# Attention over 256 heads: the last 32 query rows packed four heads to a tile, V through a staging copy, P·V metered by credits

## The chip, the core and the metric

The kernel runs on one core of a Trainium2 chip. A core has TensorE (PE in the profile; PEld is its weight load), VectorE (DVE), ScalarE (ACT), GpSimd (POOL) and SyncE (SP), which issues the DMAs here. Operands lie in SBUF, matmul results in PSUM, which has eight banks. The metric is the device time of one execution in microseconds; lower is better.

## The reference

```python
# q [8, 32, 1312, 128], k and v [8, 32, 512, 128], bf16
scale = q.shape[-1] ** -0.5
scores = jnp.einsum("bhqd,bhkd->bhqk", q, k) * scale
p = _softmax(scores, axis=-1)
return jnp.einsum("bhqk,bhkd->bhqd", p, v)
```

There are 8 x 32 = 256 independent heads, each with 1312 queries, 512 keys and a head dimension of 128.

## The kernel before

`fast_path` does all the work in a normal run. It goes through the heads in groups of eight (G = 8, 32 groups). The scores are computed transposed, keys on the partitions: for each of the four chunks of 128 keys (`c`), three matmuls of 512, 512 and 288 query columns (L145) with the transposed K chunk as weight write a score tile of 128 x 1312 over three PSUM banks; ScalarE takes the exponential of all of it, with a fixed shift instead of the row maximum, into the bf16 tile `pT` (L146). There are two such score tiles (six banks).

The second product, P·V, uses 128 columns of `pT` as weight and a chunk of V with a column of ones beside it (129 columns, tile `vp`) as the moving operand. Four chunks add up, so the output tile has 128 queries x 128 features and, in the column of ones' place, the softmax denominator. A head has eleven query tiles: ten cover queries 0 to 1279, the eleventh covers the last 128 queries, 96 of which the tenth tile has too; only its last 32 rows are stored. That makes 44 matmuls of 129 columns a head (L161). Tiles are gathered in groups, (0,1,2), (3,4,5), (6,7,8), (9,10), each in one of the two PSUM banks of the pool `ps_o`. After a group VectorE takes the reciprocal of the denominators into R (L165) and multiplies them into the output tile `om` (L167, L169) or, for the eleventh tile, `ol` (L170). At a group's end `check_group` counts the denominators that are in range.

The program is laid out by slots, four to a head. In slot s the code emits the scores and exp of chunk s mod 4 of head s div 4, and then eleven matmuls of P·V of the head that began five slots earlier (PV_LAG, PV_PER_SLOT; the generator `pv_steps`). A scheduler then sets the final order of each engine: it follows the code where everything is at hand, and takes a later instruction where it reckons that the next one must wait.

Loads go by SyncE's queue, in an order that `sp_dma` fixes. At a group's first slot `load_T` issues the next group's K, as one transposing DMA from rows of 128 elements (L100), and its Q for queries 0 to 1279, one transposing DMA a head (L110). Some slots later `load_plain` issues the 32 left-over query rows of the group after next, four heads to a tile (L73), and its V (L86), and the finished group's outputs are stored (L180, L182). The left-over rows are turned by two PE transposes a group into columns 1280 to 1311 of `qT` (L134, L135). V goes by DMA straight into `vp`, and GpSimd sets the column of ones (L83). kT and qT have two buffers, vp three.

After the heads `validity_flag` sums the counts; `exact_loop` redoes heads only if a denominator was out of range, which does not happen with these inputs.

Of the kernel before, what the change touches and what calls it, by code (L numbers as in the profile page):

```python
# [10 lines left out]
FP32 = mybir.dt.float32  # L11
# [5 lines left out]
AX = mybir.AxisListType  # L17

D, SQ, SK = 128, 1312, 512
NT = 11  # L20
QMAIN = 1280
QRANGES = ((0, 512), (512, 512), (1024, 288))
GROUPS = [(0, 1, 2), (3, 4, 5), (6, 7, 8), (9, 10)]
TILE_COL = [t * 128 for t in range(10)] + [SQ - 128]
# [3 lines left out]
P_FLUSH = 1.0e-20  # L28
G = 8


NOSYNC = mybir.DependencyInfo(mybir.DependencyClass.NoSync, mybir.DependencyReason.DATA)
PV_LAG = 5
PV_PER_SLOT = 11
QL = SQ - QMAIN
VW = 136
LB = 128 // QL


def fast_path(tc, qf, kf, vf, of, ident, R, CNT, NH):  # L40
# [4 lines left out]
    NLB = G // LB  # L45
    with ExitStack() as ctx:
        qpool = ctx.enter_context(tc.tile_pool(name="qT", bufs=2))
        kpool = ctx.enter_context(tc.tile_pool(name="kT", bufs=2))
        vpool = ctx.enter_context(tc.tile_pool(name="vpool", bufs=3))
        lpool = ctx.enter_context(tc.tile_pool(name="lpool", bufs=3))  # L50
        ptp = ctx.enter_context(tc.tile_pool(name="ptp", bufs=3))
        outp = ctx.enter_context(tc.tile_pool(name="outp", bufs=3))
        olp = ctx.enter_context(tc.tile_pool(name="olp", bufs=3))
        ps_s = ctx.enter_context(tc.tile_pool(name="ps_s", bufs=2, space=bass.MemoryType.PSUM))
        ps_o = ctx.enter_context(tc.tile_pool(name="ps_o", bufs=2, space=bass.MemoryType.PSUM))
        jpool = ctx.enter_context(tc.tile_pool(name="jpool", bufs=2))
        grp = {}
        st = {}
        pending_stores = []
        last_dma = [None]  # L60

# [13 lines left out]

        def load_V(g, j0=0, j1=G):
            if g >= NG:
                return
            h0 = g * G
            d = grp.setdefault(g, {})  # L80
            if "vp" not in d:
                vp = vpool.tile([128, G, 4, VW], BF16, tag="vp", name=f"vp{g}")
                nc.gpsimd.memset(vp[:, :, :, D:D + 1], 1.0)  # L83
                d["vp"] = vp
            vp = d["vp"]
            sp_dma(nc.sync.dma_start(vp[:, j0:j1, :, 0:D].rearrange("p j c d -> p (j c) d"),  # L86
                                     vf[h0 + j0:h0 + j1].rearrange("h (c p) d -> p (h c) d", c=4)))

        def load_plain(g):
            load_left(g)  # L90
            load_V(g)

        def load_K(g, j0=0, j1=G):
            if g >= NG:
                return
            h0 = g * G
            d = grp.setdefault(g, {})
            if "kT" not in d:
                d["kT"] = kpool.tile([128, G, SK], BF16, tag="kT", name=f"kT{g}")
            sp_dma(nc.sync.dma_start_transpose(d["kT"][:, j0:j1, :], kf[h0 + j0:h0 + j1].rearrange("h s d -> (h s) d")))  # L100

        def load_Q(g, j0=0, j1=G):
            if g >= NG:
                return
            h0 = g * G
            d = grp.setdefault(g, {})
            if "qT" not in d:
                d["qT"] = qpool.tile([128, G, SQ], BF16, tag="qT", name=f"qT{g}")
            for j in range(j0, j1):
                sp_dma(nc.sync.dma_start_transpose(  # L110
                    d["qT"][:, j, 0:QMAIN].rearrange("d (t p) -> d t p", t=10),
                    qf[h0 + j, 0:QMAIN, :].rearrange("(p t) d -> p (t d)", t=10)))

        def load_T(g):
            load_K(g)
            load_Q(g)

        def check_group(g):
            rg = R[:, g * G * NT:(g + 1) * G * NT]
            junk = jpool.tile([128, G * NT], FP32, tag="junk", name=f"junk{g}")  # L120
            nc.vector.tensor_scalar(junk[:], rg, R_LO, None, ALU.is_ge, ALU.add, accum_out=CNT[:, 2 * g:2 * g + 1])  # L121
            junk2 = jpool.tile([128, G * NT], FP32, tag="junk", name=f"junkb{g}")
            nc.vector.tensor_scalar(junk2[:], rg, R_HI, None, ALU.is_le, ALU.add, accum_out=CNT[:, 2 * g + 1:2 * g + 2])  # L123

        def flush_stores():
            for fn in pending_stores:
                fn()
            pending_stores.clear()

        def left_transpose(g):  # L130
            d = grp[g]
            tps = ps_o.tile([128, G * QL], BF16, tag="o", name=f"tl{g}")
            for b in range(NLB):
                nc.tensor.transpose(tps[:, b * 128:(b + 1) * 128], d["ql"][:, b, :], ident[:])  # L134
            nc.vector.tensor_copy(d["qT"][:, :, QMAIN:SQ], tps[:].rearrange("d (h i) -> d h i", h=G))  # L135

        def qk_exp(h, c):
            g, j = divmod(h, G)
            gd = grp[g]
            d = st.setdefault(h, {})  # L140
            if c == 0:
                d["pT"] = ptp.tile([128, 4, SQ], BF16, tag="pT", name=f"pT{h}")
            s = ps_s.tile([128, 3 * 512], FP32, tag="s", name=f"s{h}_{c}")
            for (q0, qn_) in QRANGES:
                nc.tensor.matmul(s[:, q0:q0 + qn_], lhsT=gd["kT"][:, j, c * 128:(c + 1) * 128], rhs=gd["qT"][:, j, q0:q0 + qn_], start=True, stop=True)  # L145
            nc.scalar.activation(d["pT"][:, c, :], s[:, 0:SQ], Exp, scale=scale, bias=-T0)  # L146

        def pv_steps(h):
            g, j = divmod(h, G)
            gd = grp[g]  # L150
            d = st[h]
            if j == 0:
                gd["om"] = outp.tile([128, G, 10, D], BF16, tag="om", name=f"om{g}")
                gd["ol"] = olp.tile([128, G, D], BF16, tag="ol", name=f"ol{g}")
            om = gd["om"]
            for gi, tl in enumerate(GROUPS):
                ng = len(tl)
                o = ps_o.tile([128, 3, D + 1], FP32, tag="o", name=f"o{h}_{gi}")
                for jj, t in enumerate(tl):
                    for c in range(4):  # L160
                        nc.tensor.matmul(o[:, jj, :], lhsT=d["pT"][:, c, TILE_COL[t]:TILE_COL[t] + 128], rhs=gd["vp"][:, j, c, 0:D + 1], start=(c == 0), stop=(c == 3))  # L161
                        if not (jj == ng - 1 and c == 3):
                            yield
                rr = R[:, h * NT + tl[0]:h * NT + tl[0] + ng]
                nc.vector.reciprocal(rr, o[:, 0:ng, D])  # L165
                if gi < 3:
                    nc.vector.tensor_tensor(om[:, j, tl[0]:tl[0] + ng, :], o[:, 0:ng, 0:D], rr.unsqueeze(2).to_broadcast((128, ng, D)), ALU.mult)  # L167
                else:
                    nc.vector.tensor_tensor(om[:, j, 9, :], o[:, 0, 0:D], rr[:, 0:1].to_broadcast((128, D)), ALU.mult)  # L169
                    nc.vector.tensor_tensor(gd["ol"][:, j, :], o[:, 1, 0:D], rr[:, 1:2].to_broadcast((128, D)), ALU.mult)  # L170
                    del st[h]
                    h0 = g * G
                    if g == NG - 1:
                        sp_dma(nc.sync.dma_start(of[h, 0:QMAIN, :].rearrange("(p t) d -> p (t d)", t=10), om[:, j, :, :].rearrange("p t d -> p (t d)")))
                    if j == G - 1:
                        ol = gd["ol"]
                        if g == NG - 1:
                            sp_dma(nc.sync.dma_start(of[h0:h0 + G, QMAIN:SQ, :].rearrange("h i d -> i h d"), ol[96:128, :, :]))
                        else:
                            pending_stores.append(lambda om=om, h0=h0: sp_dma(nc.sync.dma_start(  # L180
                                of[h0:h0 + G, 0:QMAIN, :].rearrange("h (p t) d -> p h (t d)", t=10), om[:].rearrange("p h t d -> p h (t d)"))))
                            pending_stores.append(lambda ol=ol, h0=h0: sp_dma(nc.sync.dma_start(  # L182
                                of[h0:h0 + G, QMAIN:SQ, :].rearrange("h i d -> i h d"), ol[96:128, :, :])))
                        check_group(g)
                        del grp[g]
                yield
# [10 lines left out]
        pv_gens = {}  # L197
        total_slots = 4 * NH + PV_LAG
        for s in range(total_slots):
# [3 lines left out]
            if has_qk and j == 0 and c == 0:  # L203
                load_T(g + 1)
            if has_qk and j == 1 and c == 2:
                load_plain(g + 2)
                flush_stores()
            if has_qk:
# [3 lines left out]
            p = s - PV_LAG  # L212
            if p >= 0:
                h, k = divmod(p, 4)
                if h < NH:
                    if k == 0:
                        pv_gens[h] = pv_steps(h)
                    gen = pv_gens[h]
                    n = PV_PER_SLOT if k < 3 else 10 ** 6
                    for _ in range(n):  # L220
                        try:
                            next(gen)
# [158 lines left out]
```

## Time and profile before

| | |
|---|---|
| median of 4 runs | 1244.09 us |
| lowest and highest | 1243.73 and 1244.12 us |
| the profiled execution's own time | 1244.43 us |
| its span, first to last instruction | 1242.7 us |
| mean granted TensorE clock | 0.999 |
| HBM over the span | 35.65 MB read, 85.98 MB written |
| DMA queue of SyncE | 239.12 MB, its packets took 86.4% of 16 engines' span |

The span is what the profiler saw between the first and the last instruction; the profiled execution took 1.7 us more. Busy time is the union of an engine's instructions. ACT's instructions overlap their neighbours, and PE's are pipelined, so that each lasts longer than the step to the next. Idle time before a group of instructions is put down to what ended it.

### The profile page before, as it was taken

The numbers are of one execution on the slowest core, as the hardware profiler recorded it, in microseconds if no ns is written. First come the engines' busy times: TensorE is split into PE (matmuls) and PEld (weight loads), VectorE is DVE, ScalarE is ACT, GpSimd is POOL, SyncE is SP. The second block draws the span as 40 slices with busy tenths as digits, with TensorE's granted clock in tenths as the row PEclk, the third lists the DMA queues.
The fourth block names the chain that finished last, engine by engine and source line by source line (L and its number), as shares of the span: only waits on it lengthen the run. The fifth ranks groups of instructions, "written<-read, shape, count | busy, mean of one in ns | idle before, by whom it ended". The sixth has DMA issues, their size and how long they took to land.

```text
span 1242.7 us, 33326 instructions
## 1 busy us (share of the span) xinstructions
PE 1213.0 (98%) x14148; PEld 923.0 (74%) x14402; DVE 734.0 (59%) x2471; ACT 1221.4 (98%) x1025; POOL 8.0 (1%) x38
## 2 busy tenths in 40 slices
PE   6999999999999999999999999999999999999998
PEld 4777777777777777777777777777777777777776
DVE  3555656556566566565665655565656565656565
ACT  6999999999999999999999999999999999999997
POOL 0000000000000000000000000000000000000000
PEclk9999999999999999999999999999999999999999
DMA  9999988889888898887998878989889988789932
GB/s 176 188 228 237 197 174 207 198 196 224 170 195 207 193 225 178 185 203 196 208 208 169 210 191 197 229 154 211 199 199 218 186 178 209 193 204 206 209 132 79
DMA packets 555064, 241.30 MB, mean 194 GB/s; under 512 B 490400, under 2 KB 522144, under 8 KB 554912
## 3 DMA queue, kind: packets, MB, share of 16 engines
q1 hardware_dynamic: 554912, 239.12, 86.4%
q8 instruction: 114, 1.87, 0.6%
q14 instruction: 38, 0.31, 0.1%
HBM read 35.65 MB, written 85.98 MB: 98 GB/s over the span
## 4 chain that ended last, share of the span: by engine, by line
PE 97%; issue 1%; DVE 0%; SPq 0%; DMA 0%; ACT 0%; DVEq 0%
PE o L161 52%; PE s L145 45%; PE tl L134 0%; DMA qT<-in_q_dram 0%; SPq L100 0%; DVE om L167 0%; SPq L73 0%; ACT pT L146 0%; DVE R L165 0%; DVE qT L135 0%; DVE om L169 0%; DVE tot_p L238 0%; PE tot L244 0%; DVE ol L170 0%; DVE junkb L123 0%
## 5 line engine op out<-in xcount | busy, mean ns | idle before, releaser
L146 ACT ACTIVATE pT<-s 128x1312 bf16<-128x1312 f32 x1024 | 1220.2, 1263 | 11.3 <-PE s L145 10.0
L161 PEld LDWEIGHTS <-pT 128*128 128x128 bf16 x11264 | 703.9, 98 | 176.1 <-DVE om L167 50.8
L161 PE MATMUL o<-vp,pT 128*128 128x129 bf16 x11264 | 813.9, 220 | 0.4 <-DVE om L167 0.2
L145 PE MATMUL s<-qT,kT 128*128 128x512 bf16 (+1 forms) x2818 | 729.8, 347 | 23.8 <-DMA qT<-in_q_dram 8.9
L167 DVE TENSOR_TENSOR om<-o,R 128x384 bf16<-128x384 f32 x768 | 427.8, 557 | 26.6
L165 DVE RECIPROCAL R<-o 128x3 f32<-128x3 f32 (+1 forms) x1024 | 179.5, 175 | 446.3 <-PE o L161 443.5
L145 PEld LDWEIGHTS <-kT 128*128 128x128 bf16 x3072 | 259.4, 98 | 129.0 <-DMA kT<-in_k_dram 7.4
L169 DVE TENSOR_TENSOR om<-o,R 128x128 bf16<-128x128 f32 x256 | 74.6, 291 | 8.9
L170 DVE TENSOR_TENSOR ol<-o,R 128x128 bf16<-128x128 f32 x256 | 71.6, 280 | 0.0
L135 DVE COPY qT<-tl 128x256 bf16<-128x256 bf16 x32 | 9.3, 291 | 21.3 <-PE tl L134 20.8
L83 POOL MEMSET vp<- 128x32 bf16 x32 | 7.5, 249 | 1116.3 <-PE o L161 1116.3
L134 PEld LDWEIGHTS <-ql 128*128 128x128 bf16 x64 | 4.3, 97 | 8.7 <-issue 8.7
L134 PE MATMUL tl<-ident,ql 128*128 128x128 bf16 x64 | 8.9, 220 | 0.0
L123 DVE TENSOR_SCALAR_CACHE_REDUCE junkb<-R 128x88 f32<-128x88 f32 x32 | 7.7, 240 | 0.0
L121 DVE TENSOR_SCALAR_CACHE_REDUCE junk<-R 128x88 f32<-128x88 f32 x32 | 7.5, 234 | 0.0
L342 DVE MEMSET R<- 128x2816 f32 x1 | 2.4, 2405 | 1.4 <-PEq L365 1.4
L123 DVE DVE_READ_ACCUMULATOR junkb<-R 128x1 f32 x32 | 2.6, 83 | 0.0
L121 DVE DVE_READ_ACCUMULATOR junk<-R 128x1 f32 x32 | 2.6, 83 | 0.0
L146 ACT ACT_TABLE_LOAD x1 | 1.3, 1283 | 0.7 <-PEq L365 0.7
L244 PE MATMUL tot<-ones,bad 128*1 128x1 f32 x2 | 0.2, 164 | 1.7 <-DVE bad L240 1.7
L244 PEld LDWEIGHTS tot<-ones,bad 128*1 128x1 f32 x2 | 0.1, 80 | 1.9 <-DVE bad L240 1.9
masks.py:199 POOL TENSOR_SCALAR_AFFINE_SELECT ident<-ident 128x128 bf16<-128x128 bf16 x1 | 0.4, 372 | 0.0
(11 smaller groups left out, 1.4 us busy)
## 6 DMA issues: line engine op xcount, KB each, us to landing
out_dram<-om SPq DMA_DIRECT2D x31, 2560.0 KB
qT<-in_q_dram SPq DMA_TRANSPOSE x256
out_dram<-om SPq DMA_DIRECT2D x8, 320.0 KB
ql<-in_q_dram SPq DMA_DIRECT2D x64, 32.0 KB
out_dram<-ol SPq DMA_DIRECT2D x32, 64.0 KB
vp<-in_v_dram SPq DMA_DIRECT2D x2, 512.0 KB
kT<-in_k_dram SPq DMA_TRANSPOSE x33
vp<-in_v_dram SPq DMA_DIRECT2D x31, 0.2 KB
```

The source lines that it names most:

```text
L83: nc.gpsimd.memset(vp[:, :, :, D:D + 1], 1.0)
L121: nc.vector.tensor_scalar(junk[:], rg, R_LO, None, ALU.is_ge, ALU.add, accum_out=CNT[:, 2 * g:2 * g + 1])
L123: nc.vector.tensor_scalar(junk2[:], rg, R_HI, None, ALU.is_le, ALU.add, accum_out=CNT[:, 2 * g + 1:2 * g + 2])
L134: nc.tensor.transpose(tps[:, b * 128:(b + 1) * 128], d["ql"][:, b, :], ident[:])
L135: nc.vector.tensor_copy(d["qT"][:, :, QMAIN:SQ], tps[:].rearrange("d (h i) -> d h i", h=G))
L145: nc.tensor.matmul(s[:, q0:q0 + qn_], lhsT=gd["kT"][:, j, c * 128:(c + 1) * 128], rhs=gd["qT"][:, j, q0:q0 + qn_], start=True, stop=True)
L146: nc.scalar.activation(d["pT"][:, c, :], s[:, 0:SQ], Exp, scale=scale, bias=-T0)
L161: nc.tensor.matmul(o[:, jj, :], lhsT=d["pT"][:, c, TILE_COL[t]:TILE_COL[t] + 128], rhs=gd["vp"][:, j, c, 0:D + 1], start=(c == 0), stop=(c ...
L165: nc.vector.reciprocal(rr, o[:, 0:ng, D])
L167: nc.vector.tensor_tensor(om[:, j, tl[0]:tl[0] + ng, :], o[:, 0:ng, 0:D], rr.unsqueeze(2).to_broadcast((128, ng, D)), ALU.mult)
L169: nc.vector.tensor_tensor(om[:, j, 9, :], o[:, 0, 0:D], rr[:, 0:1].to_broadcast((128, D)), ALU.mult)
L170: nc.vector.tensor_tensor(gd["ol"][:, j, :], o[:, 1, 0:D], rr[:, 1:2].to_broadcast((128, D)), ALU.mult)
```

## The change

The parts of it, in the order of the code:

1. The eleventh query tile is gone. A head has ten tiles in four groups, (0,1,2), (3,4,5), (6,7), (8,9), and for the second of every four heads (0,1,2), (3,4), (5,6,7), (8,9). The last 32 queries of four heads are done together: VectorE copies their 32 columns of `pT` (four chunks) of each head into a tile `pL`, and after the fourth head a block of 16 matmuls, each with a weight of 32 columns and with `tile_position` (0, 0), (0, 32), (0, 64) or (0, 96), fills one output tile of 128 rows, 32 from each head. One reciprocal and one multiplication empty it. The left-over rows are stored per four heads.
2. P·V is handed out by credits: each slot adds (4 x 10 x 4 + 7.9) / 16 = 10.49, each matmul takes 1, a left-over block 7.9; an item is emitted while the credit is at least half its cost. The lag is four slots instead of five, with an empty start one slot later.
3. Keys are numbered differently: chunk c now holds keys 4p + c, p being the partition. K comes by two transposing DMAs a group from rows of four keys (512 elements), V by one DMA a group with 1 KB runs into a staging tile `vs`, and VectorE copies it head by head into `vp`, in two of the slots of each of the last four heads of the group before (all eight ahead of the loop for the first group).
4. The starting loads are reordered (V of the whole first group after the first two heads of Q), V goes ahead of the left-over rows, the small stores ahead of the large one, and some instructions are pinned behind the last score matmul or the last multiplication in the scheduler's order.
5. R has 82 columns a group instead of 88, and `validity_flag` expects the new count. `exact_loop` only has names replaced.

```diff
+NTM = QMAIN // 128
+LB = 128 // QL
-GROUPS = [(0, 1, 2), (3, 4, 5), (6, 7, 8), (9, 10)]
+MAIN_GROUPS = ((0, 1, 2), (3, 4, 5), (6, 7), (8, 9))
+HEAD1_GROUPS = ((0, 1, 2), (3, 4), (5, 6, 7), (8, 9))
-PV_LAG = 5
-PV_PER_SLOT = 11
+PV_LAG = 4
+LEFT_COST = 7.9
...
+    slot_budget = (NC * NTM * LB + LEFT_COST) / (4.0 * LB)
...
+        def pin(inst, anchor):
+            if anchor[0] is not None:
+                tc.add_manual_dep(inst.ins, anchor[0].ins.name, NOSYNC, reason="keep pipeline position")
...
-            sp_dma(nc.sync.dma_start(vp[:, j0:j1, :, 0:D].rearrange("p j c d -> p (j c) d"),
-                                     vf[h0 + j0:h0 + j1].rearrange("h (c p) d -> p (h c) d", c=4)))
+            sp_dma(nc.sync.dma_start(d["vs"][:, j0:j1, :], vf[h0 + j0:h0 + j1].rearrange("h (p c) d -> p h (c d)", c=NC)))
+
+        def make_vp(g, j):
+            if g >= NG:
+                return
+            d = grp[g]
+            if "vp" not in d:
+                d["vp"] = vpool.tile([128, G, NC, VW], BF16, tag="vp", name=f"vp{g}")
+                nc.gpsimd.memset(d["vp"][:, :, :, D:D + 1], 1.0)
+            pin(nc.vector.tensor_copy(d["vp"][:, j, :, 0:D], d["vs"][:, j, :].rearrange("p (c d) -> p c d", c=NC)), last_dve)
...
-            sp_dma(nc.sync.dma_start_transpose(d["kT"][:, j0:j1, :], kf[h0 + j0:h0 + j1].rearrange("h s d -> (h s) d")))
+            for b in range(b0, NLB if b1 is None else b1):
+                hb = h0 + b * LB
+                sp_dma(nc.sync.dma_start_transpose(d["kT"][:, b, :, :], kf[hb:hb + LB].rearrange("h (p c) d -> (h p) (c d)", c=NC)))
...
+            groups = HEAD1_GROUPS if jb == 1 else MAIN_GROUPS
+
+            def begin():
...
+                if jb == 0:
+                    gd[f"pL{b}"] = plp.tile([128, LB, NC, QL], BF16, tag="pL", name=f"pL{g}_{b}")
+                pin(nc.vector.tensor_copy(gd[f"pL{b}"][:, jb, :, :], pT[:, :, QMAIN:SQ]), last_dve)
...
+            def left_block():
+                pL = gd[f"pL{b}"]
+                ol = gd["ol"]
+                o = ps_o.tile([128, D + 1], FP32, tag="o", name=f"oL{g}_{b}")
+                for c in range(NC):
+                    for jj in range(LB):
+                        nc.tensor.matmul(o[jj * QL:(jj + 1) * QL, :], lhsT=pL[:, jj, c, :], rhs=vp[:, b * LB + jj, c, 0:D + 1],
+                                         start=(c == 0), stop=(c == NC - 1), tile_position=(0, jj * QL))
+                rr = R[:, g, RM + b:RM + b + 1]
+                nc.vector.reciprocal(rr, o[:, D:D + 1])
+                nc.vector.tensor_tensor(ol[:, b, :], o[:, 0:D], rr.to_broadcast((128, D)), ALU.mult)
...
         load_left(0)
-        load_K(0, 0, LB)
+        load_K(0, 0, 1)
         load_Q(0, 0, 2)
-        load_V(0, 0, LB)
-        load_K(0, LB, G)
-        load_Q(0, 2, G)
-        load_V(0, LB, G)
-        load_plain(1)
+        load_V(0)
+        load_Q(0, 2, LB)
+        load_K(0, 1)
+        load_Q(0, LB, G)
+        load_V(1)
+        load_left(1)
         left_transpose(0)
+        for j in range(G):
+            make_vp(0, j)
+        queue = []
+        credit = 0.0
...
+            if has_qk and j >= G // 2 and c in (1, 3):
+                make_vp(g + 1, 2 * (j - G // 2) + c // 2)
...
+            hp, kp = divmod(s - PV_LAG, 4)
+            if kp == 0 and 0 <= hp < NH:
+                queue.extend(pv_items(hp))
+            if s > PV_LAG:
+                last_slot = s == total_slots - 1
+                if queue:
+                    credit += slot_budget
+                while queue and (last_slot or credit >= 0.5 * queue[0][0]):
+                    cost, emit = queue.pop(0)
+                    credit -= cost
+                    emit()
```

More of the change, by code (lines that the diff above doesn't have):

```diff
@@ L139, in qk_exp @@
             gd = grp[g]
[L140 removed]
             if c == 0:
[L142 removed]
+                pts[h] = ptp.tile([128, NC, SQ], BF16, tag="pT", name=f"pT{h}")
             s = ps_s.tile([128, 3 * 512], FP32, tag="s", name=f"s{h}_{c}")
[L144 to L145 removed]
@@ L149, in pv_steps, with pv_items @@
+        def pv_items(h):
             g, j = divmod(h, G)
+            b, jb = divmod(j, LB)
             gd = grp[g]
[L151 to L158, printed above, removed]
-                for jj, t in enumerate(tl):
[L160 to L186, printed above, removed]
@@ new lines, in main_mm, with emit @@
+            def main_mm(gi, jj, t, c, first, last):
+                def emit():
+                    if first:
+                        if gi == 0:
+                            begin()
+                        state["o"] = ps_o.tile([128, 3, D + 1], FP32, tag="o", name=f"o{h}_{gi}")
+                    o = state["o"]
+                    nc.tensor.matmul(o[:, jj, :], lhsT=pT[:, c, t * 128:(t + 1) * 128], rhs=vp[:, j, c, 0:D + 1],
+                                     start=(c == 0), stop=(c == NC - 1))
+                    if last:
+                        tl = groups[gi]
+                        ng = len(tl)
+                        rr = R[:, g, j * NTM + tl[0]:j * NTM + tl[0] + ng]
+                        nc.vector.reciprocal(rr, o[:, 0:ng, D])
+                        last_dve[0] = nc.vector.tensor_tensor(gd["om"][:, j, tl[0]:tl[0] + ng, :], o[:, 0:ng, 0:D],
+                                                              rr.unsqueeze(2).to_broadcast((128, ng, D)), ALU.mult)
+                        if gi == len(groups) - 1:
+                            head_done()
+                return emit
@@ L188, in fast_path @@
+            for gi, tl in enumerate(groups):
+                for jj, t in enumerate(tl):
+                    for c in range(NC):
+                        items.append((1.0, main_mm(gi, jj, t, c, first=(jj == 0 and c == 0),
+                                                   last=(jj == len(tl) - 1 and c == NC - 1))))
+            if jb == LB - 1:
+                items.append((LEFT_COST, left_block))
+            return items
         load_left(0)
-        load_K(0, 0, LB)
+        load_K(0, 0, 1)
@@ L211, in fast_path @@
                     left_transpose(g + 1)
[L212 to L222, printed above, removed]
-                        except StopIteration:
-                            break
-                    if k == 3:
-                        del pv_gens[h]
+            hp, kp = divmod(s - PV_LAG, 4)
[9 more added lines that the diff above has]
+                    emit()
+        assert not queue
         flush_stores()
@@ L335 @@
     NH = B * H
+    NG = NH // G
     qf = q.rearrange("b h s d -> (b h) s d")
```

166 lines of the change are left out of this document (97 added, 69 removed).

## The prediction

> **What bounds the kernel now.** I read the page first: the busy table, then the chain that ended last.
>
> ```profile
> span 1242.7 us, 33326 instructions
> PE 1213.0 (98%) x14148; PEld 923.0 (74%) x14402; DVE 734.0 (59%) x2471; ACT 1221.4 (98%) x1025; POOL 8.0 (1%) x38
> ...
> PE 97%; issue 1%; DVE 0%; SPq 0%; DMA 0%; ACT 0%; DVEq 0%
> ```
>
> Two engines look full, PE and ACT, but the chain is put on PE alone. The groups by line, shapes kept apart, give the durations:
>
> ```profile
> L146 ACT ACTIVATE pT<-s 128x1312 bf16<-128x1312 f32 x1024 | 1220.2, 1263 | 11.3 <-PE s L145 10.0 <-PE o L161 0.5
> L161 PE MATMUL o<-vp,pT 128*128 128x129 bf16 x11264 | 813.9, 220 | 0.4 <-DVE om L167 0.2
> L161 PEld LDWEIGHTS <-pT 128*128 128x128 bf16 x11264 | 703.9, 98 | 176.1 <-DVE om L167 50.8 <-issue 9.0
> L167 DVE TENSOR_TENSOR om<-o,R 128x384 bf16<-128x384 f32 x768 | 427.8, 557 | 26.6
> L165 DVE RECIPROCAL R<-o 128x3 f32<-128x3 f32 x768 | 138.4, 180 | 443.5 <-PE o L161 443.5
> L169 DVE TENSOR_TENSOR om<-o,R 128x128 bf16<-128x128 f32 x256 | 74.6, 291 | 8.9
> L170 DVE TENSOR_TENSOR ol<-o,R 128x128 bf16<-128x128 f32 x256 | 71.6, 280 | 0.0
> L165 DVE RECIPROCAL R<-o 128x2 f32<-128x2 f32 x256 | 41.2, 161 | 2.8
> L135 DVE COPY qT<-tl 128x256 bf16<-128x256 bf16 x32 | 9.3, 291 | 21.3 <-PE tl L134 20.8
> ```
>
> An ACTIVATE lasts 1263 ns, but 1220.2/1024 = 1.19 us is its mean share of the union, so neighbours overlap, and a late input can hide in the overlap without showing as idle time. Whether ACT could go faster is seen only where PE runs ahead, near the start (timeline, ACT alone, one row from each of three narrow windows; start, duration):
>
> ```profile
> 20.89 1.26 ACT L146 ACTIVATE pT<-s 128x1312 bf16<-128x1312 f32 x1
> 22.03 1.27 ACT L146 ACTIVATE pT<-s 128x1312 bf16<-128x1312 f32 x1
> 23.18 1.28 ACT L146 ACTIVATE pT<-s 128x1312 bf16<-128x1312 f32 x1
> ```
>
> Starts are 1.14 and 1.15 us apart: that is ACT's own pace, about 0.045 us below the 1.19 it keeps in the long run. So ACT waits, unseen, for PE. What PE does in a slot is in the chain of waits in order of time:
>
> ```profile
> 1200.15 0.62 PE o L161 x11
> 1200.77 0.55 PE s L145 x3
> 1201.33 0.69 PE o L161 x11
> 1202.01 0.55 PE s L145 x3
> 1202.57 0.62 PE o L161 x11
> ```
>
> One slot is three score matmuls (0.555 us) and eleven P·V matmuls (0.62 us, so 56.4 ns each). One slot of a head's four takes 0.07 more (the 0.69): there the next weight load waits for VectorE to free a bank (the 50.8 us in the weight-load row, most of it lost cover, not lost time). I put 0.05 on a head: 4 x (0.555 + 0.62) + 0.05 = 4.75 us, and 256 heads are 1216 us. The ends lie outside:
>
> ```profile
> 11.84 2.42 ACT L146 ACTIVATE pT<-s 128x1312 bf16<-128x1312 f32 x2 [9.81 <-PE s L145]
> ...
> 1223.99 9.51 ACT L146 ACTIVATE pT<-s 128x1312 bf16<-128x1312 f32 x8
> ```
>
> The first exp starts at 11.84 and the last ends at 1233.50: 11.8 us of head and 9.2 of tail, 21.0 together, and 1221.7 between them, 5.7 more than the heads make up.
>
> **The change, part by part.** The profiled run took 1244.43 us (span 1242.7 and 1.7 around it), 0.34 above the median of 1244.09; I sum against the run and subtract 0.3 at the end.
>
> *P·V, removed.* Each head loses the eleventh tile: 4 matmuls x 56.4 ns = 0.226 us, all on the path; 256 heads make 57.8 us.
>
> *P·V, added.* Every four heads get one block of 16 matmuls, each with a weight of 32 columns and 129 moving columns, at four column positions. No row shows one. From below, four stream at once: 4 x 56.4 = 0.225 us. From above, one after another as in L161: 16 x 56.4 = 0.90 us, and the saving is gone. I take the weight load as what limits them, the row with the nearest shape: 98 ns for 128 columns, a quarter for 32, so 16 x 24.5 = 0.39, and the last matmul, 0.056: **0.45 us**, 64 blocks, 28.8 us. Net on PE: 57.8 - 28.8 = **29.0 us saved**. The constant 7.9 in the code only places matmuls.
>
> Against this speaks a rule of the Trainium skill, "TensorEngine Tiling (Array Packing)", Key Properties: changing the tiling mode drains the array. No run here shows a drain; it is a rival below.
>
> *VectorE.* Three groups of three tiles, one of two become two of three, two of two. A scaled move of 256 columns lies between 291 ns (128) and 557 (384), so 0.42. A head's evacuation was 3 x (0.18 + 0.557) + 0.161 + 0.291 + 0.280 = 2.94 us and becomes 2 x 0.737 + 2 x 0.58 + a quarter of (0.16 + 0.28) = 2.75. New are two copies per head: 128 columns into pL and 512 columns from the staging tile into vp. The only copy row is 291 ns for 256 columns out of PSUM; I bound pL by 0.06 and 0.29 and take 0.2; vp by 0.2 and 0.7 (0.16 fixed and 1.04 ns a column, the slope between L169 and L167), and take 0.4. So VectorE goes from 734 to about 734 - 49 + 154 = 839 us, 69% of the span: no bound. But it works in order, and the pL copy waits for the head's fourth exp, the vp copy for V's landing: evacuations queue behind both, and PE waits for evacuations. The first of these waits holds nobody up for long: the scores two slots on need the bank that this exp reads, so PE can't run past it anyway. V is loaded a group ahead. The copies themselves are partly exposed. From below, even the present 0.05 a head could go: -13 us. From above, one vp copy exposed per four heads: 64 x 0.4 = +26. I take a third of a slot's present loss, 15 ns a head: **+4**.
>
> *Queues.* SP issues K as two transposes instead of one, and V ahead of the 32 left-over rows; the stores' order changes too.
>
> ```profile
> 621.76 4.27 SPq L100 DMA_TRANSPOSE kT<-in_k_dram  x1
> 626.08 14.07 SPq L110 DMA_TRANSPOSE qT<-in_q_dram  x8
> ...
> 659.93 4.28 SPq L100 DMA_TRANSPOSE kT<-in_k_dram  x1
> ```
>
> A group's transposes are issued by 640.15 (626.08 + 14.07); the next group's K, which waits for the buffer of the group just finished, is issued at 659.93, when the group loaded here begins. Some 20 us of cover hide the changed K and V loads: cost nothing; without that cover each us of late K would be a us of PE, 31 times. The waits say the same of transfers:
>
> ```profile
> PE s L145 <- DMA qT<-in_q_dram: 8.9, 1, 8.9
> PEld L161 <- DVE om L167: 50.8, 197, 0.4
> ```
>
> Scores waited for a transfer once, at the start. There the order changes most:
>
> ```profile
> 8.18 0.58 SPq L86 DMA_DIRECT2D vp<-in_v_dram  x1
> ...
> 14.20 0.42 PE L161 MATMUL o<-vp,pT 128*128 128x129 bf16 x2
> ```
>
> V of four heads was issued at 8.18 and used at 14.20. Now all eight heads land in one transfer, then VectorE copies them one by one ahead of the first evacuations: 8 x 0.4 = 3.2 us of it. Between 0 (hidden by the lag of four slots) and +5; I take **+1.5**. At the end a left-over block and its own evacuation (0.16 + 0.28) follow the last head, against a last group shorter by one matmul tile: -0.3 to +1; **+0.5**. Lag four in place of five: five slots of P·V remain after the last score either way, so nothing. Order of constants: hidden before 11.84.
>
> Sum: 1244.4 - 29.0 + 4 + 1.5 + 0.5 - 0.3 = **1221 us**. PE's slot is then 0.555 + 10 x 0.0564 + 0.45/16 + 0.016 = 1.163 us, still above ACT's 1.145: PE stays the bound, narrowly.
>
> **Rivals.**
>
> *ACT becomes the bound.* With the block at 0.225 and no VectorE stall PE needs 1.133 a slot, and ACT's 1.145 decides: 1024 x 1.145 = 1172, with 21.0 of head and tail, 1.7 around the span, 2 more at start and end and the 5.7 that the heads leave open: **1202**. For it: the three rows above. Against: the block must reach four at once. The Trainium skill, "ScalarE: Activation LUTs", What ACT_TABLE_LOAD costs, would put the bound higher: 186 ns + 0.833 a column, less 93 of overlap, an estimate of 1186 ns here; by it the time would be 1239. The three rows have 1145, and the measurement decides; I give that 0.02.
>
> *Draining around each block.* A matmul lasts 220 ns and is followed after 56, so 164 ns are in flight; emptied on entry and exit, 0.33 a block, 64 times, +21: **1242**, no change.
>
> *The bank wait moves (slower).* An evacuation holds its bank from the last matmul on. At the end, with no scores between, its length shows:
>
> ```profile
> 1234.75 0.18 DVE L165 RECIPROCAL R<-o 128x3 f32<-128x3 f32 x1 [0.21 <-PE o L161]
> 1234.96 0.56 DVE L167 TENSOR_TENSOR om<-o,R 128x384 bf16<-128x384 f32 x1
> 1235.58 0.17 PEld L161 LDWEIGHTS <-pT 128*128 128x128 bf16 x3 [0.30 <-DVE om L167]
> ```
>
> 0.83 from the reciprocal to the next weight load, and 0.16 in flight before: 1.0 us, or 0.86 for two tiles. Two banks alternate, so the group between must last that long. Laying the matmuls out by the credits (10, 11, 10, 11 ... to a slot), every group has scores beside it but one: tiles 8 and 9 of each first head, 8 matmuls, 0.45 us. The next head's first matmul would wait 0.86 - 0.45 = 0.41, 64 times: 26 us, **1247**, slower. It decides from 0.36 us a block on, the 23 us forecast over 64. Against it: the program is not run in code order where a bank is late.
>
> ```profile
> 608.37 0.27 PE L134 MATMUL tl<-ident,ql 128*128 128x128 bf16 x2
> 608.48 0.33 PE L161 MATMUL o<-vp,pT 128*128 128x129 bf16 x3
> 608.66 0.59 PE L145 MATMUL s<-qT,kT 128*128 128x512 bf16 x2
> 609.09 0.61 PE L161 MATMUL o<-vp,pT 128*128 128x129 bf16 x8
> ```
>
> Here two score matmuls of the next slot stand inside a slot's eleven, pulled forward past the transposes' evacuation. The same would fill the 0.41.
>
> *The column positions do not overlap.* The block takes 0.90: +28.8, **1250**.
>
> **How the numbers follow.** The forecast (1212 to 1235) gets 0.50; ACT as the bound, 1201 to 1212, 0.18; the page's pace and mixtures between 1235 and 1241.6, 0.07; drains and partial bank waits, 1241.6 to 1246.6, 0.10; the bank wait in full 0.08; no overlap 0.07. What a measurement of this kernel can tell from no change is about 0.2%, 2.5 us. So faster 0.75, same 0.10, slower 0.15. The range goes from the ACT bound, 1201, to the bank wait, 1247; about 0.15 lies outside, mostly above.
>
> **What would show it.** In the profile after: the 16 small matmuls of a block spread over 0.45 us (0.9: no overlap; a gap of 0.16 at each side: drains); slots of 1.16 with PE still the chain; ACT starts rarely 1.145 apart. A row of PE or its weight loads waiting for the evacuation at far over 50 us, or VectorE copies standing ahead of evacuations in it, speaks for the bank wait. Scores waiting for a transfer after the start, or a first exp later than 12, would make the queue part wrong.

## The result and the profile after

| | before | after |
|---|---|---|
| median | 1243.93 us (12 runs beside it) | 1217.19 us (8 runs) |
| span of the profiled execution | 1242.7 us | 1215.3 us |
| first exp starts | 11.84 | 12.14 |
| last exp ends | 1233.50 | 1206.56 |

The ratio is 0.9785, with a 95% interval of 0.9775 to 0.9795: faster by 2.1%, where 1221 us had been forecast. Times below are medians of executions at a granted TensorE clock of 0.98 or more; one execution, of the kernel without block and transposes, took 1503 us at 0.755 and is left out. The page after, in the parts shown of before:

```profile
span 1215.3 us, 33796 instructions
PE 1185.0 (98%) x14147; PEld 889.5 (73%) x14402; DVE 793.9 (65%) x2855; ACT 1191.9 (98%) x1025; POOL 8.0 (1%) x38
...
PE 97%; issue 1%; SPq 1%; DMA 1%; DVE 0%; ACT 0%
```

ACT's busy time fell with PE's, by 29.5 and 28.0 us, though not one exp has changed: it was following PE. PE is still what the chain is put on. The groups by line, shapes apart (busy us, mean ns, then idle before):

```profile
L152 ACT ACTIVATE pT<-s 128x1312 bf16<-128x1312 f32 x1024 | 1190.6, 1266 | 13.9 <-PE s L150 10.7
L185 PEld LDWEIGHTS <-pT 128*128 128x128 bf16 x10240 | 661.0, 98 | 164.4 <-DVE om L192 19.6 <-issue 6.5
L192 DVE TENSOR_TENSOR om<-o,R 128x256 bf16<-128x256 f32 x512 | 217.2, 424 | 17.5
L105 DVE COPY vp<-vs 128x512 bf16<-128x512 bf16 x256 | 71.9, 283 | 2.9 <-DMA vs<-in_v_dram 2.9
L176 DVE COPY pL<-pT 128x128 bf16<-128x128 bf16 x256 | 46.8, 183 | 1.4 <-ACT pT L152 1.4
L210 PEld LDWEIGHTS <-pL 128*32 128x32 bf16 x1024 | 15.0, 95 | 16.7 <-issue 13.1 <-DVE om L192 0.2
```

The two new copies take 283 and 183 ns (0.4 and 0.2 us had been put on them), the move of two tiles 424 ns (0.42 us). VectorE stands at 65%. What PE does with a left-over block is in the timeline of PE (start, duration, line, operation, count; a row's duration includes the depth of the pipe, so steps are read from the starts):

```profile
614.19 0.33 PE L185 MATMUL o<-vp,pT 128*128 128x129 bf16 x3
614.46 0.41 PE L210 MATMUL oL<-vp,pL 128*32 128x129 bf16 x16
614.80 0.73 PE L150 MATMUL s<-qT,kT 128*128 128x512 bf16 x3
```

Three P·V matmuls at 0.056 end their turn at 614.36; the block starts 0.10 later and the scores at 614.80. So a block takes **0.44 us**, gap included, against a forecast of 0.45. It fits only if several stream at once: 16 x 0.056 alone would be 0.90. The entry is no wait for a bank: the step from the last P·V matmul to the block is 0.150 us in the trace, and just as long in the run below that leaves out VectorE's reciprocal. And where the bank of the next head's first tile comes free late, the order is this:

```profile
600.24 0.71 PE L185 MATMUL o<-vp,pT 128*128 128x129 bf16 x9
600.78 0.59 PE L150 MATMUL s<-qT,kT 128*128 128x512 bf16 x2
601.21 0.28 PE L185 MATMUL o<-vp,pT 128*128 128x129 bf16 x2
601.33 0.29 PE L150 MATMUL s<-qT,kT 128*128 128x288 bf16 x1
```

Nine P·V matmuls (the last of tile 7 and the eight of tiles 8 and 9), then two score matmuls of the next slot pulled forward, and only then the two that need the bank. Nobody waits 0.41 here. The nine take 0.54 where 9 x 0.056 is 0.51: about 0.03 is lost where a short group follows a long one.

### The profile page after: what moved, and what is told of

Its sections match the earlier page's. It is cut to its first block, busy times and chain, and to the rows that moved or that the text cites. A ratio compares the mean times of both kernels' runs of the same rounds, so it can differ in the third digit from the quotient of the medians.

```text
span 1215.3 us, 33796 instructions
## 1 busy us (share of the span) xinstructions
PE 1185.0 (98%) x14147; PEld 889.5 (73%) x14402; DVE 793.9 (65%) x2855; ACT 1191.9 (98%) x1025; POOL 8.0 (1%) x38
## 4 chain that ended last, share of the span: by engine, by line
PE 97%; issue 1%; SPq 1%; DMA 1%; DVE 0%; ACT 0%
PE o L185 49%; PE s L150 46%; PE oL L210 2%; PE tl L140 1%; DMA vs<-in_v_dram 1%; SPq L116 0%; SPq L126 0%; DVE om L192 0%; SPq L86 0%; ACT pT L152 0%; DVE R L191 0%; DVE vp L105 0%; DVE ol L214 0%; DVE tot_p L297 0%; PE tot L303 0%
## 5 line engine op out<-in xcount | busy, mean ns | idle before, releaser
L152 ACT ACTIVATE pT<-s 128x1312 bf16<-128x1312 f32 x1024 | 1190.6, 1266 | 13.9 <-PE s L150 10.7
L185 PEld LDWEIGHTS <-pT 128*128 128x128 bf16 x10240 | 661.0, 98 | 164.4 <-DVE om L192 19.6
L185 PE MATMUL o<-vp,pT 128*128 128x129 bf16 x10240 | 766.4, 220 | 0.7 <-DVE om L192 0.4
L192 DVE TENSOR_TENSOR om<-o,R 128x384 bf16<-128x384 f32 (+1 forms) x1024 | 502.5, 491 | 35.2
L105 DVE COPY vp<-vs 128x512 bf16<-128x512 bf16 x256 | 71.9, 283 | 2.9 <-DMA vs<-in_v_dram 2.9
L176 DVE COPY pL<-pT 128x128 bf16<-128x128 bf16 x256 | 46.8, 183 | 1.4 <-ACT pT L152 1.4
L210 PEld LDWEIGHTS <-pL 128*32 128x32 bf16 x1024 | 15.0, 95 | 16.7 <-issue 13.1
L210 PE MATMUL oL<-vp,pL 128*32 128x129 bf16 x1024 | 26.3, 223 | 0.0
L214 DVE TENSOR_TENSOR ol<-oL,R 128x128 bf16<-128x128 f32 x64 | 18.7, 292 | 1.1
L213 DVE RECIPROCAL R<-oL 128x1 f32<-128x1 f32 x64 | 10.1, 157 | 0.0
```

The lines of the kernel that those rows point to most:

```text
L105: pin(nc.vector.tensor_copy(d["vp"][:, j, :, 0:D], d["vs"][:, j, :].rearrange("p (c d) -> p c d", c=NC)), last_dve)
L152: nc.scalar.activation(pts[h][:, c, :], s[:, 0:SQ], Exp, scale=scale, bias=-T0)
L176: pin(nc.vector.tensor_copy(gd[f"pL{b}"][:, jb, :, :], pT[:, :, QMAIN:SQ]), last_dve)
L185: nc.tensor.matmul(o[:, jj, :], lhsT=pT[:, c, t * 128:(t + 1) * 128], rhs=vp[:, j, c, 0:D + 1], start=(c == 0), stop=(c == NC - 1))
L192: last_dve[0] = nc.vector.tensor_tensor(gd["om"][:, j, tl[0]:tl[0] + ng, :], o[:, 0:ng, 0:D], rr.unsqueeze(2).to_broadcast((128, ng, D)), ...
L210: nc.tensor.matmul(o[jj * QL:(jj + 1) * QL, :], lhsT=pL[:, jj, c, :], rhs=vp[:, b * LB + jj, c, 0:D + 1], start=(c == 0), stop=(c == NC - ...
```

## The experiments

Eleven kernels, each the changed kernel with one edit, compared with the kernel before on the same chip. The ratio to read them against is 0.9785 (1217.2 us).

**What paces a block: the order in it.**

```diff
-                for c in range(NC):
-                    for jj in range(LB):
+                for jj in range(LB):
+                    for c in range(NC):
                         nc.tensor.matmul(o[jj * QL:(jj + 1) * QL, :], lhsT=pL[:, jj, c, :], ...
```

> The two loops of the left-over block are swapped: each column position's four matmuls stand in a row. Theory A (the four positions stream at once, 0.25 us a block, and entering and leaving the narrow mode costs 0.19): in a row 16 x 0.057 + 0.19 = 1.1 us instead of 0.44, 64 blocks, about +42, 1259 us. Theory B (the prediction's: the narrow weight loads, one after another, set the pace at 0.45 a block): the order doesn't matter, 1217. Theory C (at once, but no price for the mode): 0.90 instead of 0.44, +29, 1246.

Measured: 1219.77 us, ratio 0.9805 (0.979 to 0.982). None of the three: it costs 2.6 us, 0.04 a block. Timeline of PE around such a block:

```profile
616.17 0.33 PE L185 MATMUL o<-vp,pT 128*128 128x129 bf16 x3
616.43 0.44 PE L210 MATMUL oL<-vp,pL 128*32 128x129 bf16 x16
616.81 0.73 PE L150 MATMUL s<-qT,kT 128*128 128x512 bf16 x3
```

From start to the scores 0.38 instead of 0.34. Four matmuls in a row at one column position do not hold back those at the next. So the order within sixteen hardly matters. That alone would fit the prediction's reading, weight loads one after another; the next run separates them.

**What paces a block: the moving columns.**

```diff
-                        nc.tensor.matmul(o[jj * QL:(jj + 1) * QL, :], ..., rhs=vp[:, b * LB + jj, c, 0:D + 1],
+                        nc.tensor.matmul(o[jj * QL:(jj + 1) * QL, 64:D + 1], ..., rhs=vp[:, b * LB + jj, c, 64:D + 1],
```

> The left-over block's matmuls take only moving columns 64 to 128 (65 instead of 129); features 0 to 63 of the last 32 queries are left at zero. Theory A (four positions stream at once, the stream sets the pace of 47 to 57 ns per four): the steps between fours fall to about 30, the block by 0.09 us, 64 blocks, -6, 1211 us. Theory B (the narrow weight loads set the pace): the steps stay at 47 to 57, 1217. In both the 94 and 96 ns at entry and exit stay.

Measured: 1214.52 us, ratio 0.9766 (0.9752 to 0.9779). Timeline of PE:

```profile
612.79 0.33 PE L185 MATMUL o<-vp,pT 128*128 128x129 bf16 x3
613.05 0.31 PE L210 MATMUL oL<-vp,pL 128*32 128x65 bf16 x16
613.29 0.73 PE L150 MATMUL s<-qT,kT 128*128 128x512 bf16 x3
```

From its start to the scores, with the same sixteen weight loads, the block falls from 0.34 to 0.24, and the gap ahead of it stays (612.79 + 0.17 to 613.05, 0.09). The weight loads are not the pace; the stream of four at a time is. Only 2.7 of the 6.4 us that 64 blocks save here reach the end (below).

**The price of going in and out.**

```diff
-LEFT_COST = 7.9
+LEFT_COST = 12.2
...
-    slot_budget = (NC * NTM * LB + LEFT_COST) / (4.0 * LB)
+    slot_budget = (NC * NTM * G + LEFT_COST) / (4.0 * G)
...
+                for bb in range(NLB):
+                    pL = gd[f"pL{bb}"]
+                    for c in range(NC):
+                        for jj in range(LB):
...
-            if jb == LB - 1:
+            if j == G - 1:
                 items.append((LEFT_COST, left_block))
```

> The two left-over blocks of a group stand together: 32 narrow matmuls, one reciprocal and one multiplication, once in eight heads. Theory A (0.19 us for entering and leaving the narrow mode, whatever the block's length): 32 pairs of switches fewer, -6 us, 1211. Theory B (the pace is the weight loads', no price for the mode): 1217. If a burst of twice the length makes ACT wait for scores for longer than PE's lead, some of it comes back: up to 32 x 0.25 = +8.

Measured: 1228.48 us, ratio 0.9879 (0.9864 to 0.9895): 11 us slower than the changed kernel. Timeline of PE around the double block:

```profile
619.10 0.72 PE L150 MATMUL s<-qT,kT 128*128 128x512 bf16 x3
619.74 0.64 PE L211 MATMUL oL<-vp,pL 128*32 128x129 bf16 x32
620.31 0.73 PE L150 MATMUL s<-qT,kT 128*128 128x512 bf16 x2
```

From its start to the scores 32 matmuls take 0.57 us, where 16 take 0.34: sixteen more cost 0.23, and 0.11 is paid once for leaving. With the 0.10 for entering that is theory A: two single blocks are 0.88, the double one 0.67, 0.21 saved in a group. It is lost again at the start of the next group (timeline, PE and its weight loads):

```profile
614.34 0.72 PE L150 MATMUL s<-qT,kT 128*128 128x512 bf16 x3
614.89 1.03 PE L185 MATMUL o<-vp,pT 128*128 128x129 bf16 x11
615.29 0.45 PEld L185 LDWEIGHTS <-pT 128*128 128x128 bf16 x8 [0.24 <-ACT pT L152]
615.97 0.50 PE L150 MATMUL s<-qT,kT 128*128 128x512 bf16 x2
```

Eleven P·V matmuls, 0.62 elsewhere, take 1.08 up to the next scores: after three of them PE waits for the exp of the last chunk of keys. A slot brings 10.38 credits, so four bring 41.5, and a head's 40 matmuls leave some over: the heads' first matmuls come earlier and earlier until the block after the eighth, and the exp they need is not done. The trace agrees: behind the first exp of the seventh head, the eighth and the next group's first, ACT's next exp ends 1.21, 1.27 and 1.38 us later (medians over the groups), where the changed kernel has 1.16, 1.18 and 1.16. Not the burst, as I had feared, but the pacing around it takes back more than the switches give.

**The bank wait of the rival.** Each PE instruction from the second group on is tied to the one before it in the code:

```diff
+        def chain(inst):
+            if in_order[0] and last_mm[0] is not None:
+                tc.add_manual_dep(inst.ins, last_mm[0].ins.name, NOSYNC, reason="code order")
+            last_mm[0] = inst
+            return inst
...
+            in_order[0] = s >= 4 * G
```

> From the second group on every PE instruction is held to the order of the code, so two P.V matmuls that stood after two pulled-forward score matmuls go back ahead of them. Theory A (the bank wait of the prediction's rival): the next head's first matmul waits 0.41 us for its bank once in four heads, 64 times, +26, 1243 us. Theory B (PE has slack there, or the evacuation is quicker than summed): within 3 us of 1217.

Measured: 1251.66 us, ratio 1.0065 (1.0049 to 1.008): slower than the kernel before. Timelines of PE and of VectorE at the place:

```profile
596.64 0.71 PE L194 MATMUL o<-vp,pT 128*128 128x129 bf16 x9
597.59 0.29 PE L194 MATMUL o<-vp,pT 128*128 128x129 bf16 x2 [0.24 <-DVE om L201]
```

```profile
596.90 0.17 DVE L200 RECIPROCAL R<-o 128x2 f32<-128x2 f32 x1 [0.24 <-PE o L194]
597.10 0.42 DVE L201 TENSOR_TENSOR om<-o,R 128x256 bf16<-128x256 f32 x1
```

Nine matmuls end their turn at 597.15 (596.64 + 9 x 0.056); the tenth starts at 597.59, 0.07 after VectorE is done at 597.52: a wait of 0.44, where 0.41 had been worked out. 64 of them are 28 us of the 34.5. Most of the rest lies at the transposes, where the block now waits for VectorE to copy the turned rows (list of waits: PE 6.3 us in 30 waits). So the rival's mechanism is real, and the scheduler's order is what keeps it out of the changed kernel.

**The second head's split.**

```diff
-HEAD1_GROUPS = ((0, 1, 2), (3, 4), (5, 6, 7), (8, 9))
+HEAD1_GROUPS = MAIN_GROUPS
```

> The second of every four heads takes its ten tiles as 3, 3, 2, 2 like the others instead of 3, 2, 3, 2; its third group then has no scores beside it. Theory A (a score matmul pulled forward fills the gap, as it does at the first head): within 3 us of 1217. Theory B (the wait of 0.41 us for a bank appears in full): 64 x 0.41, 1243.

Measured: 1223.4 us, ratio 0.983 (0.9815 to 0.9845): between the two. The scheduler pulls two score matmuls forward here as well, but not all of the wait goes:

```profile
608.40 0.59 PE L150 MATMUL s<-qT,kT 128*128 128x512 bf16 x2
608.97 0.23 PE L185 MATMUL o<-vp,pT 128*128 128x129 bf16 x1
```

Two score matmuls fill 0.43 (2 x 0.216), to 608.83; 0.14 is left. The extra split is worth 6.2 us, 0.097 a block.

**The loads and copies of K and V.**

```diff
+            sp_dma(nc.sync.dma_start(d["vp"][:, j0:j1, :, 0:D].rearrange("p j c d -> p (j c) d"),
+                                     vf[h0 + j0:h0 + j1].rearrange("h (c p) d -> p (h c) d", c=NC)))
...
-            pin(nc.vector.tensor_copy(d["vp"][:, j, :, 0:D], ...), last_dve)
...
+            sp_dma(nc.sync.dma_start_transpose(d["kT"][:, j0:j1, :], kf[h0 + j0:h0 + j1].rearrange("h s d -> (h s) d")))
```

> K and V are loaded as before the change (K as one transposing DMA a group, V by DMA straight into vp), with no staging tile and no VectorE copies of V; all else as after it. Theory A (the copies are hidden, the waits for banks are set by the tile groups alone): 1217, within 2. Theory B (the prediction's: 256 copies of 512 columns are partly exposed, with pL 15 ns a head): 1213 to 1215. Theory C (the wide runs of the new loads relieve the DMA engines and that is worth time): slower, 1220 or more.

Measured: 1217.06 us, ratio 0.9786 (0.9772 to 0.9799). No difference: the wider runs and the 256 copies of V (72 us of VectorE), taken together, do not touch the end. The run takes both away at once, so a gain of one and a loss of the other that cancel are not excluded.

**What comes next after PE.** The block left out altogether:

```diff
-LEFT_COST = 7.9
+LEFT_COST = 0.0
...
-                o = ps_o.tile([128, D + 1], FP32, tag="o", name=f"oL{g}_{b}")
...
-                nc.vector.tensor_tensor(ol[:, b, :], o[:, 0:D], rr.to_broadcast((128, D)), ALU.mult)
+                nc.gpsimd.memset(ol[:, b, :], 0.0)
```

> The left-over block, its pL copies and its evacuation are left out (the last 32 queries of each head are stored as zeros). Theory A (ACT's own pace of 1.145 us a slot is the next bound): 1024 x 1.145 = 1172, with 12.1 before the first exp, 8.7 after the last, 1.9 around the span and 32 x 0.21 for the transposes: 1202 us, with ACT's starts 1.144 apart nearly everywhere. Theory B (ACT can go on following PE): PE's slot falls by 0.44/16 = 0.027, 28 us, 1189.

Measured: 1216.0 us, ratio 0.9773 (0.9758 to 0.9789): 28 us of PE's work are gone and 1.2 of time. ACT's starts, from the timeline of ACT in narrow windows:

```profile
607.74 1.36 ACT L151 ACTIVATE pT<-s 128x1312 bf16<-128x1312 f32 x1
608.88 1.37 ACT L151 ACTIVATE pT<-s 128x1312 bf16<-128x1312 f32 x1
```

The starts are 1.14 us apart, as theory A has them. But each exp also lasts about 12 ns longer than the one before, so the ends are further apart than the starts. A row over a long window gives the pace of the ends (timeline of ACT from one group's transposes to the next, this run and then the changed kernel):

```profile
597.42 37.12 ACT L151 ACTIVATE pT<-s 128x1312 bf16<-128x1312 f32 x32
```

```profile
597.02 37.20 ACT L152 ACTIVATE pT<-s 128x1312 bf16<-128x1312 f32 x32
```

The first exp of each row lasts 1.26, so the other 31 end (37.12 - 1.26) / 31 = **1.157 us** apart here and 1.159 in the changed kernel. So ACT's own pace is 1.157, not 1.145, and between the transposes the changed kernel is already at it: taking work from PE can gain some 2 us there, 1024 x 0.002. With 1024 x 1.157 = 1185 in place of 1172, theory A's sum is 1214.

What ACT still loses lies in the main once a group at the transposes (ACT, two narrow windows, then PE):

```profile
594.69 2.63 ACT L151 ACTIVATE pT<-s 128x1312 bf16<-128x1312 f32 x2
597.42 1.26 ACT L151 ACTIVATE pT<-s 128x1312 bf16<-128x1312 f32 x1
```

```profile
595.80 0.27 PE L139 MATMUL tl<-ident,ql 128*128 128x128 bf16 x2
595.91 0.28 PE L181 MATMUL o<-vp,pT 128*128 128x129 bf16 x2
596.22 0.59 PE L149 MATMUL s<-qT,kT 128*128 128x512 bf16 x2
596.65 0.61 PE L181 MATMUL o<-vp,pT 128*128 128x129 bf16 x8
597.10 0.29 PE L149 MATMUL s<-qT,kT 128*128 128x288 bf16 x1
```

ACT's last exp ends at 597.32 and the next begins at 597.42, without overlap, and ends 1.36 after the last one: 0.20 above ACT's pace. Its third score matmul stands behind eight P·V matmuls in the fixed order and starts only at 597.10. The changed kernel has the same step, 1.37, so 31 x 0.21 = 6.5 us of its time are lost there.

The transposes and the loads of the left-over rows taken out, first in the kernel without the block, then with the block in (in both, the left-over columns of qT are zeros):

```diff
+                nc.gpsimd.memset(d["qT"][:, :, QMAIN:SQ], 0.0)
...
-                if c == 0 and j == G - 3 and g + 1 < NG:
-                    left_transpose(g + 1)
```

> As in the run without the left-over block, and the two PE transposes a group that turn the left-over query rows are left out too (those columns of qT are zeros). Theory A (ACT's pace of 1.144 us is the wall there, and the only large loss is one step of 1550 ns a group at the transposes, 0.41 above it): 31 x 0.41 = -12.6, about 1203 us, with the four steps of 1175 to 1178 a group left. Theory B (the step belongs to something else that comes once a group: stores, loads, the counts): 1214 or more.

Measured: 1207.34 us, ratio 0.9704 (0.9686 to 0.9722): 8.7 us less than without the block alone, where 12.6 had been expected. The 0.41 of theory A was read from starts; in the ends the step is 0.20, and 31 of them are 6.4 us. That is about what went between the first exp and the last (1194.3 to 1187.7 us); the rest goes with an earlier first exp, 8.45 instead of 11.41. What is left, 1187.7, is 1024 x 1.157 = 1184.8 and 3 us at the start: after its start this kernel runs at ACT's pace throughout.

> The changed kernel with the left-over block, without the two PE transposes a group (the left-over columns of qT are zeros, so the last 32 queries are wrong). Theory A (PE sets the end in nearly every slot): ACT's step of 1376 becomes 1171, 31 x 0.21 = -6.4, 1211 us. Theory B (ACT's pace already flattens what PE saves, as with half the columns, where 2.7 of 6.7 came through): 1214 to 1216.

Measured: 1209.89 us, ratio 0.9727 (0.9713 to 0.974): -7.3 us, theory A. Part of it is again the earlier first exp, 8.27 instead of 12.14. From the start of exp 33 to that of exp 992, thirty groups, it is 1111.9 us instead of 1118.0: 6.1 for 30 x 0.21, so the step at the transposes comes through in full.

**The evacuation made shorter.**

```diff
-                        nc.vector.reciprocal(rr, o[:, 0:ng, D])
```

> The reciprocal of the main tiles is left out and R stays at 1.0, so these outputs are not divided by the softmax sum; VectorE frees a bank some 0.2 us earlier. Theory A (the five places a block where matmuls step 80 and 67 ns instead of 56, 34 ns together, are waits for a bank): they vanish, 64 x 5 x 0.034 = -11, 1206 us. Theory B (they belong to the change of tile group itself, not to VectorE): 1217.

Measured: 1214.96 us, ratio 0.9769 (0.9754 to 0.9785): 2.2 of the 11 us. The waits of PE's weight loads for VectorE do go. The list of waits of the changed kernel has them (us, times, longest), and the groups by line of this run no longer do:

```profile
PEld L185 <- DVE om L192: 19.6, 66, 0.4
```

```profile
L152 ACT ACTIVATE pT<-s 128x1312 bf16<-128x1312 f32 x1024 | 1188.1, 1337 | 13.4 <-PE s L150 10.6
L185 PEld LDWEIGHTS <-pT 128*128 128x128 bf16 x10240 | 669.0, 98 | 152.9 <-issue 2.1 <-ACT pT L152 0.5
```

The other row says why so little arrives: an exp lasts 1337 ns in the mean instead of 1266, because its scores are ready while the one before still runs, and ACT's 1188.1 us are within 4 of 1024 x 1.157. PE has caught up with ACT. The scheduler's order changed too, so the 8.8 us that do not arrive are not split to the last.

**The left-over rows turned by DMA.**

```diff
+                sp_dma(nc.sync.dma_start_transpose(d["qT"][:, j, QMAIN:SQ], qf[h0 + j, QMAIN:SQ, :]))
...
-                    left_transpose(g + 1)
```

> The 32 left-over rows of a head are turned by a transposing DMA of their own straight into qT; the two PE transposes a group, VectorE's copy of them and their loads go. Theory A (the transposes cost 0.21 us a group on the path, seen as ACT's one step of 1376 among 1144 to 1171): 32 x 0.21 = -6.6, 1210.5 us. Theory B (256 more transposing DMAs delay Q on engines that are 87% busy): scores wait for qT, 1217 or more.

Measured: 1277.9 us, ratio 1.0269 (1.0254 to 1.0283). Theory B's side, by another way. The first rows of the waits that are new:

```profile
DVE vp L105 <- DMA vs<-in_v_dram: 77.0, 25, 10.8
PEld L186 <- DVE om L193: 73.7, 89, 4.1
ACT pT L153 <- PE s L151: 72.6, 34, 6.6
```

SyncE's queue shows why (timeline of SP):

```profile
575.28 14.31 SPq L116 DMA_TRANSPOSE kT<-in_k_dram  x2
...
599.56 1.40 SPq L127 DMA_TRANSPOSE qT<-in_q_dram  x1
601.01 1.22 SPq L126 DMA_TRANSPOSE qT<-in_q_dram  x1
...
615.46 14.13 SPq L116 DMA_TRANSPOSE kT<-in_k_dram  x2
```

Turning 32 rows (L126) keeps the queue for 1.22 us, turning 1280 (L127) for 1.40. Eight more a group are 10 us. The changed kernel's queue stands still for 14 us behind the large store before it takes the next group's K, and K then takes 4.32 or 5.66 (at 608.60 and 645.91 of its timeline); here K follows the store at once and takes 14, and no run shows what holds it. So the queue hardly rests, and from one group's K to the next it needs 40.2 us, where a group of the changed kernel lasts 37.3. It falls further behind with each group: V's load, issued 18 us after its group's first exp in the changed kernel, comes 38 us after it in the second group here and 54 in the ninth. From there VectorE's copy waits for V, the evacuations wait in order behind the copy, and PE for them. That is the cover that the prediction counted on, used up.

## Why the prediction was right

**What bounds the kernel.** Right for the kernel before: PE, with ACT following. The size of ACT's slack was misread. The three rows have starts 1.14 and 1.15 apart, but they also last 1.26, 1.27 and 1.28, so their ends are 1.15 and 1.16 apart, and over 31 steps ACT's pace is 1.157. The slack was 0.035 us a slot, not 0.045. In the changed kernel PE still hardly ever waits for an exp (the list of waits has two, 1.1 and 0.2 us), but "narrowly" is more true than was meant: the mean slot is 1.166, near the forecast 1.163, ACT's pace is 1.157, and between the transposes next to nothing is left. A fifth of ACT's starts, 201 of 1023, are within 1.14 to 1.15 of the one before, where "rarely" was the sign to look for. The estimate of 1186 ns worked out from the Trainium skill ("ScalarE: Activation LUTs", What ACT_TABLE_LOAD costs) does not hold here; the ends are 1157 apart. The time given for that estimate was added up short: with the 5.7 us that the sum of 1202 has, it is 1245, not 1239.

**P·V.** The forecast had 29.0 us; the rows after give 57.8 - 64 x 0.44 = 29.6. The size was right, the reason wrong. "I take the weight load as what limits them" falls with the run on half the columns: four positions stream at once, as in the lower bound, and the other 0.19 is spent going in and out. That was the rival's mechanism, at 0.10 a side instead of 0.164. Two misreadings cancelled, which is luck. The rule of the Trainium skill, "TensorEngine Tiling (Array Packing)", Key Properties, that a change of tiling mode drains the array, agrees with the gap of 0.10 us ahead of each block; whether it is a drain or a weight load that can't run ahead no run shows.

**VectorE, +4.** It was about +2, and not by the copies: they are shorter than put, and taken away together with the wide loads they change nothing (0.9786 against 0.9785). It is the waits for banks. Over thirty groups, from exp 33 to exp 992, the trace has longer steps than usual at P·V matmuls that add up to 10.4 us, 9.7 before; and the first transpose of a group, which needs a bank too, starts 0.226 us after the last score matmul, 0.177 before. Together they cost 2.2 us more. In the run without the reciprocal the transpose's step falls to 0.122, so it is VectorE that it waits for.

**Start and end, +2.** The first exp came 0.3 later (12.14 against 11.84), and from the last exp to the end it is 8.7 instead of 9.2 us: together -0.2. A first exp after 12 was to be a sign against the queue part; but seven of the runs above keep these starting loads, and theirs comes at 11.2 to 11.6, so the 0.3 is this execution's own.

With these the sum would have been 1244.4 - 29.6 + 2.2 - 0.2 - 0.3 = 1216.5, against 1217.2. Measured between first and last exp is 1221.7 - 1194.4 = 27.3, and 29.6 - 2.2 is 27.4.

**The rivals.** The bank wait: right in mechanism, place and size (0.44 against 0.41), kept away by the pulled-forward scores as argued. No overlap: wrong; it is nearly full overlap. ACT as the bound at 1202: the step that failed is "1024 x 1.145". With the pace of the ends, 1.157, it is 1185, and the rival's own sum becomes 1215. Two kernels that took PE well below ACT's pace came to 1216 and 1207, the second without the transposes and with an earlier first exp. So forecast and rival lie 6 us apart, and the time alone, 1217, does not tell them apart; the changed kernel stands close to both bounds.

**Queues.** Right: next to no wait for transfers after the start (six short ones for the left-over rows, 1.9 us in all), and no effect of K's and V's new loads taken together. The cover was real but not wide: turning the left-over rows by DMA, 8 x 1.22 us more a group, used it up.

## What to carry to other kernels

Where two engines are both at 98%, find a stretch where one runs free (here ACT with scores waiting) and compare its pace there with its pace in the long run; the difference is what the other engine may save before the bound changes. Read the pace from the ends over many instructions, not from a few starts: here starts 1.144 apart hid ends 1.157 apart, and 1024 of them are 13 us. Count the gain of a later saving place by place, not over the total: 28 us less work on PE gained 1.2, because ACT was late only at the transposes. And an in-order engine that frees banks must not queue a copy whose input can be late ahead of evacuations.

## What the runs showed of the hardware

A weight load of 32 columns lasts 95 ns in its row, as long as one of 128 (98), and yet sixteen narrow matmuls with their loads go through in about 0.25 us (0.44 less 0.10 for going in and 0.10 for going out). Four narrow matmuls in a row at one column position cost only 0.04 us a block more than four at four positions. A transposing DMA of 32 rows holds its queue almost as long as one of 1280 (1.22 and 1.40 us). Where their scores are ready early, exps start 1.144 us apart and end 1.157 apart, each lasting some 12 ns longer than the one before.
